# A gated layer by seven block products in place of eight, its last 64 tokens turned

## The chip, the cores and the metric

The kernel runs on one core of a Trainium2 chip. The metric is the device time of one execution in microseconds, taken as the median of three runs. A smaller number is better.

## The reference

Three layers follow each other: attention over a window of 128 tokens, a ReLU layer with a normalization ahead of it, and a gated layer. The change is in the gated layer alone. There are 4 batches (B) of 576 tokens (S), 512 features (DM), and 512 features in each half of the wide layer (DG).

```python
def _moe2_ref(x, w_in, g_ln, w_sg, b_sg, w_out):
    h = x @ w_in                      # (4, 576, 512) @ (512, 1024)
    h = gelu_tanh(h)
    u, v = (h[..., :512], h[..., 512:])
    v_n = (v - mean(v)) / np.sqrt(var(v) + 1e-06) * g_ln
    v_s = np.einsum('ts,bsd->btd', w_sg, v_n) + b_sg[None, :, None]
    gated = u * v_s
    return x + gated @ w_out
```

`gelu_tanh`, `mean` and `var` stand here for the lines that write them out. Below, the four products are called V and U (the two halves of `x @ w_in`), S (the product with `w_sg`, the gate) and O (the product with `w_out`).

## The kernel before

Every large product is made from numbers that are split into a high part (fp32r, names ending in h) and a low part (the rest, names ending in l). A product then has three terms, high by high, high by low and low by high, so each 128 by 128 block of weights meets its data three times. A split costs one ScalarE copy for the high part and one two-input subtraction for the low part.

Attention and the ReLU layer (called phase 1 here) are put in order by a planner, `Sched`: every piece of work is an `Op` with an engine, a cost, a priority, needs and buffers, and the planner writes the instructions in the order in which it thinks they can start. The order on each engine is then fixed in the program. The ReLU layer works on groups of 256 tokens; `m1` (L891) and `m2` (L902) alternate in pieces of 24 matmuls of 256 columns.

The gated layer (phase 2, class `Phase2`) is written out by hand. `play` runs chunks in a given order: V in 18 tiles of 128 tokens (24 matmuls of 256 columns, L1155), U in 16 chunks (24 matmuls, of 256 and 320 columns in turn, L1215), S in 16 chunks of 28 such matmuls (L1230) and O in 16 of 24 (L1257). `early_v` puts V tiles between the last pieces of phase 1. Around them stand GELU (L1201, L1217), the statistics and the normalization of V (L1186 to L1192), the splits (`split`, L1144 on ScalarE, L1145 on GpSimd), the gate (L1234, L1235), the last addition (L1262) and the DMA out (L1263), of which the last chunk makes two, of 320 and of 256 tokens. Weights come in as 64-bit numbers and are turned into high and low parts by `Split64` jobs that `tick` spreads over the chunks. Transfers are issued by SP.

Of the kernel before, what the change touches and what calls it, by code (L numbers as in the profile page):

```python
# [106 lines left out]
def split64(jobs, stage, out=None):  # L107

    for n, j in enumerate(jobs):
        if stage == 0:  # L110
# [17 lines left out]

class Sched:
# [105 lines left out]
def phase1(tc, nc, a, x2d, cst, p2):  # L235
# [599 lines left out]
    def evac(g, j, half, q):  # L835
# [10 lines left out]
        if (g, j) in final:  # L846
            yield Op("SP", 500, q - 1000, token=("xd", g, half), size=2 ** 18)
            sync.dma_start(out=x2d[g][:, zs], in_=x[:, zs])
            if half == 1:
                yield Op(None, 0, 0, need=[("xd", g, 0), ("xd", g, 1)], token=("x2", g))  # L850

    def moe():
        for n, (f, (g, j)) in enumerate(steps):
# [98 lines left out]
    def end_attention():  # L952
# [3 lines left out]
        p2.ps_v = tc.alloc_tile_pool(name="ps_v", bufs=2, space=PSUM, side="right", reuse_waits="tile")  # L956
        p2.open_0()
        sched.done["p2", "wv"] = sched.now
        p2.ps_e = tc.alloc_tile_pool(name="ps_e", bufs=2, space=PSUM, side="right", reuse_waits="tile")
        for n, j in enumerate(list(p2.queue)):  # L960
            sched.spawn(p2.flow(sched, j, n), sched.now)
        for i in range(4):
            sched.spawn(p2.early_v(i, when[2, stream[-1]] + EPRI[i]), sched.now)

# [9 lines left out]
    sched.run("end")  # L974
    for p in (ps_a, ps_h, wps.pop(), np_, cp):
        p.release()
    p2.run(xt[G - 1], (xp, hp))


class Job:  # L980

    def __init__(self, p2, label, name, at, src, shape):
        self.p2, self.label, self.name, self.at, self.src, self.shape, self.stage = p2, label, name, at, src, shape, 0

    def load(self):
        self.s = self.p2.sp.tile([128, 512], I64, tag="st", name="st", bufs=NS2)
        if self.shape:
            self.s = self.s.bitcast(F32)[:, :int(np.prod(self.shape))]  # L990
            if len(self.shape) == 2:
                self.s = self.s.rearrange("p (a b) -> p a b", a=self.shape[0])
        self.p2.nc.sync.dma_start(out=self.s, in_=self.src)

    def step(self):

        if (self.shape or self.stage == 4) and not hasattr(self.p2, self.name):
            return False
        if self.shape:
            self.p2.split(*self.out(), self.s)  # L1000
            return True
        if self.stage == 0:
            self.j = [Split64(self.p2.nc, self.p2.sp, NC2, self.s)]
# [386 lines left out]
```

## Time and profile before

| what | value |
|---|---|
| median of three runs | 732.79 us (732.0 to 733.34) |
| the profiled execution's own time | 731.82 us |
| its span in the profile | 730.1 us |
| TensorE busy | 714.3 us, 98% of the span |
| VectorE busy | 440.0 us, 60% |
| ScalarE busy | 288.5 us, 40% |
| GpSimd busy | 240.4 us, 33% |
| mean granted clock of TensorE | 0.994 |

The span is what the profiler sees between the first and the last instruction; the time of the execution is 1.7 us more. In a row of the chain of waits the first number is the start, the second how long the piece held the chain, then the engine, the tile that it wrote, the line and the number of instructions. In a group a duration is the mean of one instruction, which for matmuls holds their overlap with the next one, so that the pace of matmuls is read from the chain and not from there.

### The profile page before, as it was taken

To read this page: it belongs to the slowest core of one execution; us is meant where nothing else is said; L and a number is where in the kernel's file an instruction comes from. 1 tells how busy PE (TensorE), PEld (TensorE's weight loads), DVE (VectorE), ACT (ScalarE), POOL (GpSimd) and SP (SyncE) were. 2 spreads that over 40 slices of the span, in tenths; PEclk is the share of its full clock that TensorE was granted. 3 is DMA by queue.
4 is the path that set the end of the run, shared out by engine and by line. 5 is a ranking of instruction groups with operands and counts; after the bars stand their busy time and mean duration, and the time that the engine had idled before them with its cause. 6 is when DMAs were issued, how large, how long until landed. Compare 5 with 4: busy or idle time off the path is not lost.

```text
span 730.1 us, 16607 instructions
## 1 busy us (share of the span) xinstructions
PE 714.3 (98%) x6678; PEld 686.9 (94%) x6678; DVE 440.0 (60%) x1202; ACT 288.5 (40%) x762; POOL 240.4 (33%) x291
## 2 busy tenths in 40 slices
PE   6889999999999999999999999999999999999997
PEld 3568999999999999999999999999999999999997
DVE  6999989889782673764744738737325315314232
ACT  5887664545532422522424425124423123223210
POOL 1445251334411321312313233026637217326220
PEclk8999999999999999999999999999999999999999
DMA  8564532033221110112022253305310240250002
GB/s 297 176 209 133 173 121 80 28 94 94 78 87 31 56 51 24 49 58 59 19 69 70 54 165 103 117 29 167 115 64 1 73 137 17 69 175 2 1 33 97
DMA packets 51627, 63.45 MB, mean 87 GB/s; under 512 B 10336, under 2 KB 38880, under 8 KB 51552
## 3 DMA queue, kind: packets, MB, share of 16 engines
q1 hardware_dynamic: 51552, 62.41, 27.2%
q8 instruction: 52, 0.85, 0.5%
q14 instruction: 23, 0.19, 0.1%
HBM read 52.96 MB, written 9.44 MB: 85 GB/s over the span
## 4 chain that ended last, share of the span: by engine, by line
PE 88%; DVE 6%; ACT 3%; DMA 1%; issue 1%; SPq 0%; DVEq 0%; ACTq 0%
PE acc L902 25%; PE ps_h L891 25%; PE ps_s L1230 8%; PE ps_o L1257 7%; PE ps_u L1215 7%; PE ps_v L1155 7%; PE s L476 2%; PE o L661 1%; PE o L617 1%; PE tps L617 1%; ACT t L527 1%; DVE sc L96 1%; PE tps L661 1%; DMA st<-in_w 1%; DVE sc L99 1%
## 5 line engine op out<-in xcount | busy, mean ns | idle before, releaser
L832 DVE SCALAR_TENSOR_TENSOR hl<-ps_h,hh 128x512 fp32r<-128x512 f32 x72 | 49.6, 689 | 84.8 <-ACT hh L830 84.5
L902 PE MATMUL acc<-hh,w2h 128*128 128x256 f32 x576 | 92.5, 283 | 0.0
L891 PE MATMUL ps_h<-xh,w1h 128*128 128x256 f32 x576 | 91.5, 281 | 0.0
L891 PE MATMUL ps_h<-xh,w1l 128*128 128x256 f32 x576 | 90.0, 278 | 0.0
L891 PE MATMUL ps_h<-xl,w1h 128*128 128x256 f32 x576 | 90.0, 278 | 0.0
L902 PE MATMUL acc<-hh,w2l 128*128 128x256 f32 x576 | 89.9, 278 | 0.0
L902 PE MATMUL acc<-hl,w2h 128*128 128x256 f32 x576 | 89.9, 278 | 0.0
L830 ACT ACTIVATE hh<-ps_h 128x512 fp32r<-128x512 f32 x72 | 42.9, 595 | 117.4 <-PE ps_h L891 116.9
L485 POOL TENSOR_SCALAR_AFFINE_SELECT m<-m 128x256 f32<-128x256 f32 (+1 forms) x88 | 41.2, 475 | 124.7 <-ACT m L566 123.1
L891 PEld LDWEIGHTS ps_h<-xh,w1h 128*128 128x128 f32 x576 | 77.1, 188 | 1.2 <-issue 1.1
L902 PEld LDWEIGHTS acc<-hh,w2h 128*128 128x128 f32 x576 | 77.3, 189 | 0.1
L902 PEld LDWEIGHTS acc<-hh,w2l 128*128 128x128 f32 x576 | 77.1, 188 | 0.0
L891 PEld LDWEIGHTS ps_h<-xh,w1l 128*128 128x128 f32 x576 | 77.1, 188 | 0.0
L891 PEld LDWEIGHTS ps_h<-xl,w1h 128*128 128x128 f32 x576 | 77.0, 188 | 0.0
L902 PEld LDWEIGHTS acc<-hl,w2h 128*128 128x128 f32 x576 | 76.9, 188 | 0.0
L527 ACT ACTIVATE t<-t,sm 128x128 f32<-128x128 f32 x144 | 56.1, 392 | 23.4 <-DVE sm L521 22.6
L535 POOL TENSOR_TENSOR t<-t,sm 128x256 f32<-128x256 f32 x47 | 29.6, 629 | 73.4 <-DVE sm L531 53.2
L1234 DVE SCALAR_TENSOR_TENSOR gt<-ps_s,g,bb 128x576 f32<-128x576 f32 x16 | 13.1, 818 | 62.4 <-PE ps_s L1230 62.4
L1145 POOL TENSOR_TENSOR gl<-gt,gh 128x576 fp32r<-128x576 f32 x16 | 23.4, 1466 | 56.4 <-ACT gh L1144 56.4
L87 ACT ACTIVATE sc<-st 128x512 f32<-128x512 f32 (+1 forms) x52 | 30.7, 599 | 20.8 <-DMA st<-in_w 7.6
L99 DVE SCALAR_TENSOR_TENSOR sc<-st,sc 128x512 int32<-128x512 int32 (+1 forms) x52 | 35.6, 691 | 0.2
L96 DVE SCALAR_TENSOR_TENSOR sc<-st,sc 128x512 int32<-128x512 int32 (+1 forms) x52 | 32.7, 637 | 0.2
(177 smaller groups left out, 1561.6 us busy)
## 6 DMA issues: line engine op xcount, KB each, us to landing
st<-in_w SPq DMA_DIRECT2D x24, 512.0 KB, 4.1
x2d<-x SPq DMA_DIRECT2D x18, 256.0 KB, 2.0
out<-xr SPq DMA_DIRECT2D x15, 288.0 KB, 2.1
st<-in_w SPq DMA_DIRECT2D x16, 256.0 KB, 2.6
st<-in_wi SPq DMA_DIRECT2D x8, 512.0 KB, 4.2
st<-x2d SPq DMA_DIRECT2D x8, 512.0 KB, 5.0
xr<-x2d SPq DMA_DIRECT2D x8, 512.0 KB, 7.2
rq<-in_q SPq DMA_DIRECT2D x28, 128.0 KB, 3.0
```

What stands on the lines that cost most here:

```text
L96: dve.scalar_tensor_tensor(out=xi, in0=self.wh, scalar=-0x40000000, in1=xi, op0=ALU.bitwise_and, op1=ALU.bitwise_or)
L99: dve.scalar_tensor_tensor(out=xi, in0=self.wl, scalar=29, in1=xi, op0=ALU.logical_shift_right, op1=ALU.bitwise_or)
L485: pool.affine_select(out=out, in_=in_, pattern=pat, compare_op=ALU.is_ge, fill=0.0, base=-1 if up else 0, channel_multiplier=1 if up else -1)
L527: act.activation(out=t[:, h], in_=t[:, h], func=ACTF.Exp, bias=st[:, h:h + 1], scale=-1.0, accum_out=sums[:, h, 0:1])
L830: act.activation(out=h, in_=ps, func=ACTF.Relu)
L832: dve.scalar_tensor_tensor(out=l, in0=ps, scalar=0.0, in1=h.bitcast(F32), op0=ALU.max, op1=ALU.subtract)
L891: pe.matmul(ps[:, half], w[:, kc, f], m[:, kc], start=kc == 0 and x == 0, stop=kc == 3 and x == 2)
L902: pe.matmul(accs[half][:, d], w[:, f, ds], m[:, k], start=fi and d == 0 and k == 0 and x == 0, stop=la and k == 1 and x == 2, skip_group_c ...
L1155: self.nc.tensor.matmul(ps[:, cs], xs[s][:, kc, c0:c0 + 128], self.wv[m][:, kc, cs], start=kc == 0 and x == 0 and z == 0, stop=kc == 3 and ...
L1215: pe.matmul(ps[:, c], wu[s][:, kc, ds], self.x[m][:, kc, c], start=kc == 0 and x == 0, stop=kc == 3 and x == 2)
L1230: pe.matmul(ps[:, c], l, r[:, c], start=n == 0, stop=n == len(mm) - 1)
L1257: pe.matmul(ps[:, c], wo[s][:, kc, ds], gated[b][m][:, kc, c], start=n == 0, stop=n == 11)
```

## The change

A batch's first 512 tokens and its 512 features are seen as 2 by 2 blocks of 256. V, U and S are made by seven products of sums of such blocks (`PA` and `PB` name the sum of either side, `CHAIN` the order and the PSUM bank), each of 12 matmuls of 256 columns with the three terms. For that the weights and the data are mixed: for every one of the seven sums, additions (L1160), a high part (L1149) and a low part (L1152), the last two lines on ScalarE and on VectorE or GpSimd. Three of the seven products are copied out of PSUM by ScalarE into a room called `te` (L1397), and three are then added on to such a copy by VectorE (L1403); the seventh output is read from PSUM itself.

The 64 tokens that are left of each batch go in other ways. V and U compute them for all four batches together (`v_tail` L1465, `u_tail` L1501, 48 matmuls each, called Vt and Ut). In S, `rest` adds their rows of V to four of the products (L1330, 4 matmuls each). The gate's last 64 rows are computed transposed (`narrow`, L1573 to L1575, 18 matmuls), copied by ScalarE (L1585) and turned back by four fp32 matmuls of 64 columns with a matrix `J` (L1590). O works by groups of 256 tokens, 48 matmuls each; its ninth group is the four times 64 tokens, whose result is sent by DMAs of 64 tokens (L1680).

Phase 2 is now planned by `Sched` too, in the order V0 U0 Vt V1 U1 V2 U2 V3 U3 Ut S0 S1 O0 O1 S2 O2 O3 S3 O4 to O8. Memory is handed out as rooms (`stock`, `take`): X, V and Y rooms for blocks, `te` rooms for sums, `tt` rooms for additions. Six of the Y rooms lie in the memory of the weights of U (`more`) and are handed out when the last product of U3 has been issued. The table of GELU on ScalarE is loaded at the end of attention in place of ahead of V's first tile, O's weights are loaded later, and S's mixed weights lie where V's were.

```diff
+PA = {1: 0, 2: 1, 3: 5, 4: 2, 5: 3, 6: 4, 7: 6}
+PB = {1: 0, 2: 1, 3: 2, 4: 5, 5: 3, 6: 4, 7: 6}
+CHAIN = ((1, "X"), (2, "Z"), (6, "X"), (5, "Y"), (7, "X"), (3, "Y"), (4, "X"))
+TERMS = (0, 0), (0, 1), (1, 0)
...
+        self.order = [("V", 0), ("U", 0), ("Vt", 0)] + [(k, b) for b in range(1, B) for k in "VU"] + [("Ut", 0)]
+        self.order += [("S", 0), ("S", 1), ("O", 0), ("O", 1), ("S", 2), ("O", 2), ("O", 3), ("S", 3)]
+        self.order += [("O", g) for g in range(4, G)]
...
+    def split(self, h, l, src, w, pri, take=(), need=(), make=None, both=True):
...
+        self.nc.scalar.activation(out=h, in_=src, func=ACTF.Copy)
+        o = Op(None, 0, pri, alt=[("POOL", 150 + 2.15 * w, 0)] + [("DVE", 64 + 1.05 * w, DVE2, 1)] * both)
+        yield o
+        self.by(o).tensor_tensor(out=l, in0=src, in1=h.bitcast(F32), op=ALU.subtract)
...
+        for e in range(2):
+            for kt in range(2):
+                for s, m in TERMS:
+                    pe.matmul(ps[:, e], l[s][:, kt, 128 * e:128 * e + 128], r[m][:, kt],
+                              start=fresh and e == 0 and kt == 0 and s == m, stop=kt == 1 and s == 1, skip_group_check=True)
...
+        after = {6: ("e", n, 1), 7: ("e", n, 6), 3: ("e", n, 5), 4: ("a", n, 7)}
+        for k, (P, bk) in enumerate(CHAIN):
...
+            if P == 4 and (kind, b) == ("U", B - 1):
+                for z in "hl":
+                    t = self.pu.tile([128, 3584], F32R, tag="wu" + z, name="more", bufs=1)
+                    for k in range(3):
+                        q = S.stock.setdefault("Y", [])
+                        tok = ("stock", "Y%d" % len(q))
+                        S.done[tok] = S.free["PE"] + HOPP
...
+    def evac(self, kind, b, n, P, ps, te):
+        o = Op("ACT", 490, self.pri(kind, b, -90), need=[("P", kind, b, P)], take=[("te", 1, ("tef", n, P))], token=("e", n, P))
+        yield o
+        te[P] = self.get(o.got[0], [128, 2, 256], F32, "te")
+        self.nc.scalar.activation(out=te[P], in_=ps, func=ACTF.Copy)
...
+        if g < G - 1:
+            yield Op("SP", 500, pri, token=("od", g, i), size=2 ** 18)
+            self.nc.sync.dma_start(out=self.a["out"][b, :, z, 256 * j:256 * j + 256], in_=xr[:, z])
+        else:
+            yield Op("SP", 2000, pri, token=("od", g, i), size=2 ** 18)
+            for b in range(B):
+                self.nc.sync.dma_start(out=self.a["out"][b, :, z, 512:S_], in_=xr[:, z, 64 * b:64 * b + 64])
```

Three places in the program show what this does to the order. A row gives the line, the operation, what it writes and reads, its shape, and the engine on which it waits, if any.

First, ScalarE's order between the last product of U and the first of S. In the kernel before, on the way from U to S of batch 0, GELU of U (`u`) and of V's last tile (`vg`) stand between splits of V (`vnh`, `vt`), and the gate's split (`gh`) comes next:

```order
L1217 ACTIVATE u_7439<-ps_u_7440 128x576 [waits PE_49]
L1144 ACTIVATE vnh_7329<-vg_7415 128x512 [waits DVE_49]
L1217 ACTIVATE u_7439<-ps_u_7474 128x576 [waits PE_49]
L1201 ACTIVATE vg_7528<-ps_v_7503 128x512 [waits PE_49,Pool_49]
L1217 ACTIVATE u_7439<-ps_u_7531 128x576 [waits PE_49]
L1144 ACTIVATE vt0_7020<-vg_7528 64x512 [waits DVE_49]
L1144 ACTIVATE vt1_7021<-vg_7528 64x512
L1217 ACTIVATE u_7439<-ps_u_7562 128x576 [waits PE_49]
L1144 ACTIVATE gh_7593<-gt_7624 128x576 [waits DVE_49]
L1144 ACTIVATE x2h_7016<-st_7627 128x4x256 [waits DMAHW2_49]
```

In the changed kernel, between U3 and S0, `more` is a block of batch 1 of V in U's weights' memory, `bN` a block of normalized V, `tt` and `mx` sums of data and of weights, `wvh` the mixed weights of S, and `te_8632` the copy of S0's first product:

```order
L1149 ACTIVATE more_8501<-v_7601 128x512 [waits PE_49]
L1149 ACTIVATE bN_8539<-tt_8537 128x512 [waits DVE_49]
L1149 ACTIVATE more_8501<-v_7601 128x512
L1149 ACTIVATE wvh_6270<-mx_8443 128x2x256 [waits DVE_49]
L1149 ACTIVATE bN_8573<-tt_8546 128x512 [waits DVE_49]
L1448 ACTIVATE v_8198<-v_8198,ag_8386 128x512
L1149 ACTIVATE bN_8581<-tt_8579 128x512 [waits DVE_49]
L1420 ACTIVATE v_8596<-te_8334 128x2x256
L1420 ACTIVATE v_8596<-te_8318 128x2x256
L1420 ACTIVATE u_8597<-te_8403 128x512
L1420 ACTIVATE u_8598<-te_8464 128x512 [waits PE_49]
L1420 ACTIVATE u_8597<-psU_8372 128x512
L1420 ACTIVATE u_8598<-te_8445 128x512
L1397 ACTIVATE te_8632<-psS_8583 128x512 [waits PE_49,Activation_49]
L1149 ACTIVATE bN_8636<-tt_8623 128x512 [waits DVE_49]
```

The first row waits for TensorE, because Ut still reads U's weights: it is released by Ut's last matmuls. Five more splits, the normalization of a V room and six GELUs stand behind it, and behind those the copy of S0's first product (`psS_8583`). The kernel before has no such copy, and no row here that waits for an earlier reader of a buffer on TensorE.

Second, TensorE's order at the start of S. In the kernel before, U's last matmuls are followed by those of S, whose only waits are for V's splits:

```order
L1215 MATMUL ps_u_7562<-x2h_7016,wuh_6872 128x320
L1215 MATMUL ps_u_7562<-x2l_7017,wuh_6872 128x256
L1215 MATMUL ps_u_7562<-x2l_7017,wuh_6872 128x320
L1215 MATMUL ps_u_7562<-x2h_7016,wul_6873 128x256
L1215 MATMUL ps_u_7562<-x2h_7016,wul_6873 128x320
L1230 MATMUL ps_s_7595<-wsh_7162,vnh_7329 128x256 [waits Activation_49]
L1230 MATMUL ps_s_7595<-wsh_7162,vnh_7329 128x320
L1230 MATMUL ps_s_7595<-wsl_7163,vnh_7329 128x256
L1230 MATMUL ps_s_7595<-wsl_7163,vnh_7329 128x320
L1230 MATMUL ps_s_7595<-wsh_7162,vnl_7330 128x256 [waits Pool_49]
```

In the changed kernel this is the end of S0's second product (into bank `psS_8606`, its last three matmuls those of `rest`) and the start of its third, product 6, into the bank of the first:

```order
L1330 MATMUL psS_8606<-kh_8122,vt0_7342 128x256
L1330 MATMUL psS_8606<-kl_8123,vt0_7342 128x256
L1321 MATMUL psS_8583<-wvh_6270,bN_8573 128x256 [waits Activation_49]
L1321 MATMUL psS_8583<-wvl_6271,bN_8573 128x256
L1321 MATMUL psS_8583<-wvh_6270,bN_8573 128x256 [waits DVE_49]
L1321 MATMUL psS_8583<-wvh_6270,bN_8573 128x256
L1321 MATMUL psS_8583<-wvl_6271,bN_8573 128x256
```

Product 6 waits for ScalarE, which must have copied `psS_8583` out first (the row `te_8632` above), and for VectorE, which makes the low part of `bN_8573`.

Third, SP's order at the end. In the kernel before, the last DMAs send 576 tokens of 128 features each, and the last chunk in two pieces:

```order
L1263 DMA out_0<-xr_8801 128x576 [waits DMAHW6_49,DVE_49]
L1263 DMA out_0<-xr_8801 128x576 [waits DVE_49] x2
L1263 DMA out_0<-xr_9056 128x576 [waits DMAHW3_49,DMAHW4_49,DMAHW2_49,DVE_49]
L1263 DMA out_0<-xr_9056 128x576 [waits DVE_49] x2
L1263 DMA out_0<-xr_9056 128x320 [waits DVE_49]
L1263 DMA out_0<-xr_9056 128x256 [waits DMAHW5_49,DVE_49]
```

In the changed kernel they send 256 tokens of 256 features, and for the ninth group 64 tokens of 256 features, four for each half of the features:

```order
L1676 DMA out_0<-xr_9680 128x2x256 [waits DVE_49]
L1680 DMA out_0<-xr_9736 128x2x64 [waits DMAHW6_49,DMAHW4_49,DVE_49]
L1680 DMA out_0<-xr_9736 128x2x64 [waits DMAHW5_49]
L1680 DMA out_0<-xr_9736 128x2x64
L1680 DMA out_0<-xr_9736 128x2x64 [waits DMAHW7_49]
L1680 DMA out_0<-xr_9736 128x2x64 [waits DMAHW0_49,DVE_49]
L1680 DMA out_0<-xr_9736 128x2x64 [waits DMAHW1_49]
L1680 DMA out_0<-xr_9736 128x2x64 [waits DMAHW2_49]
L1680 DMA out_0<-xr_9736 128x2x64 [waits DMAHW3_49]
```

Behind the last addition there is one DMA in the kernel before; now there are four.

## Rows read from the trace of the kernel before

**Rows 1.** The page: busy us of each engine, share of the span, instructions
```profile
PE 714.3 (98%) x6678; PEld 686.9 (94%) x6678; DVE 440.0 (60%) x1202; ACT 288.5 (40%) x762; POOL 240.4 (33%) x291
```

**Rows 2.** The chain of waits, 480 to 731 us: start us, us, engine, tile, line, instructions
```profile
by line: PE ps_s L1230 23.5%; PE ps_o L1257 20.2%; PE ps_u L1215 20.2%; PE ps_v L1155 20.0%; PE acc L902 7.9%; PE ps_h L891 6.5%; DVE xr L1262 0.2%; DVEq L1386 0.1%; issue 0.0%
...
513.21 2.74 PE ps_v L1155 x24
515.95 2.83 PE acc L902 x24
518.78 8.18 PE ps_v L1155 x72
...
542.43 14.75 PE ps_s L1230 x112
557.18 5.66 PE ps_v L1155 x48
...
701.12 25.30 PE ps_o L1257 x192
...
726.44 0.49 DVE xr L1262
726.92 0.33 DVEq L1386
```

**Rows 3.** Timeline of VectorE, 518 to 520 us: start us, us, instruction
```profile
518.82 0.69 DVE L841 TENSOR_TENSOR et<-acc,rstd 128x512 f32<-128x512 f32 x1 [0.72 <-PE acc L902]
519.42 1.28 DVE L845 TENSOR_TENSOR x<-x,et 128x512 f32<-128x512 f32 x2
```

**Rows 4.** Timeline of ScalarE at 553 us
```profile
553.08 0.69 ACT L1144 ACTIVATE gh<-gt 128x576 fp32r<-128x576 f32 x1 [3.63 <-DVE gt L1235]
553.67 1.04 ACT L1144 ACTIVATE x2h<-st 128x1024 fp32r<-128x1024 f32 x1
```

**Rows 5.** Groups of ScalarE, 513 to 730 us: count, busy us, mean ns of one
```profile
L1144 ACT ACTIVATE vnh<-vg 128x512 fp32r<-128x512 f32 x16 | 10.1, 630 | 29.8 <-DVE vg L1192 29.8
...
L1201 ACT ACT_TABLE_LOAD x1 | 1.3, 1283 | 0.0
```

**Rows 6.** Groups of GpSimd, 513 to 730 us
```profile
L1145 POOL TENSOR_TENSOR vnl<-vg,vnh 128x512 fp32r<-128x512 f32 x16 | 20.8, 1302 | 28.3 <-ACT vnh L1144 28.3
```

**Rows 7.** Groups of VectorE, 513 to 730 us
```profile
L1235 DVE TENSOR_TENSOR gt<-gt,u 128x576 f32<-128x576 f32 x16 | 21.4, 1340 | 1.1
...
L1262 DVE TENSOR_TENSOR xr<-xr,ps_o 128x576 f32<-128x576 f32 x15 | 11.3, 754 | 26.6 <-PE ps_o L1257 26.6
```

**Rows 8.** Timeline at 550 us, VectorE beside GpSimd
```profile
550.01 2.41 POOL L1145 TENSOR_TENSOR x2l<-st,x2h 128x1024 fp32r<-128x1024 f32 x1
...
550.70 2.35 DVE L1235 TENSOR_TENSOR gt<-gt,u 128x576 f32<-128x576 f32 x1
```

**Rows 9.** Windows: window, its length, busy us of PE, PEld, DVE, ACT, POOL, PEclk, DMA, GB/s
```profile
8.00:12.00 4.00, 0.34 (x3) 0.20 (x2) 3.21 (x22) 2.98 (x14) 0.61 (x1) 1.00 1.00 359
12.00:16.00 4.00, 3.62 (x37) 1.88 (x36) 3.55 (x17) 3.60 (x13) 2.02 (x4) 0.50 1.09 385
16.00:20.00 4.00, 3.24 (x16) 1.79 (x16) 2.35 (x15) 2.46 (x11) 0.80 (x3) 0.64 0.93 343
...
44.00:48.00 4.00, 2.09 (x19) 1.21 (x15) 3.93 (x13) 3.57 (x11) 1.65 (x2) 1.00 0.46 115
```

**Rows 10.** Timeline of TensorE, 7 to 13 us, with the idle time before
```profile
11.69 0.44 PE L617 MATMUL tps<-ident,t 128*128 128x128 f32 x2 [3.66 <-POOL t L535]
```

**Rows 11.** Timeline of SP's queue, 725 to 730 us
```profile
726.95 0.81 SPq L1263 DMA_DIRECT2D out<-xr  x2
```

**Rows 12.** DMA issues of the whole run: KB each, median us from issue to landing
```profile
st<-x2d SPq DMA_DIRECT2D x8, 512.0 KB, 5.0
...
out<-xr SPq DMA_DIRECT2D x1, 128.0 KB, 1.8
```

**Rows 13.** Groups of TensorE, whole run: the nearest fp32 matmul
```profile
L723 PE MATMUL ps_ln<-x,ones 128*128 128x256 f32 x8 | 1.9, 379 | 0.0
```

More of the change, by code (lines that the diff above doesn't have):

```diff
@@ L848, in evac @@
             sync.dma_start(out=x2d[g][:, zs], in_=x[:, zs])
+            sched.done["xi", g, half] = sched.now
             if half == 1:
@@ L955, in end_attention, with end_relu @@
             p.release()
[L956 to L963, printed above, removed]
+        p2.begin = ("m1", *stream[-1], 1)
+        p2.open_0(sched)
+    def end_relu():
+        yield Op(None, 0, 0, need=["end", ("xi", G - 1, 0), ("xi", G - 1, 1)])
+        for p in (ps_a, ps_h, wps.pop(), np_, cp, xp, hp):
+            p.release()
+        p2.open_4()
     for e in units:
@@ L973, in phase1 @@
         sched.spawn(gen)
[L974 to L1003, printed above, removed]
[L1004 to L1012 removed]
+    sched.run("finished")
+    p2.close()
+S_ = S
+PA = {1: 0, 2: 1, 3: 5, 4: 2, 5: 3, 6: 4, 7: 6}
+PB = {1: 0, 2: 1, 3: 2, 4: 5, 5: 3, 6: 4, 7: 6}
+CHAIN = ((1, "X"), (2, "Z"), (6, "X"), (5, "Y"), (7, "X"), (3, "Y"), (4, "X"))
+TERMS = (0, 0), (0, 1), (1, 0)
+MM = 113.4
+DVE2 = 100
 class Phase2:
@@ new lines, in tail_v @@
+    def tail_v(self, z, ps, pri):
+        tok = ("vtf", z)
+        o = Op("ACT", 565, pri, need=[("P", "Vt", 0, z)], take=[("te", 1, tok)], token=("bk", "Vt", z))
+        yield o
+        t = self.get(o.got[0], [128, 1, DG], F32, "te")
+        self.nc.scalar.activation(out=t[:, 0], in_=ps.rearrange("p e c -> p (e c)"), func=GELU)
+        yield from self.norm(t, 1, ("vn", z), pri)
+        yield Op(None, 0, pri, need=[("vn", z)])
+        for y in range(2):
+            o = self.vt[2 * z + y] = self.vts[2 * z + y]
+            hi, lo = slice(64 * y, 64 * y + 64), slice(64 - 64 * y, 128 - 64 * y)
+            yield from self.split(o[hi], o[lo], t[hi, 0], 512, pri, both=False)
+            self.sched.done["vt", 2 * z + y] = self.sched.free[self.last] + HOP
+            self.used(tok, 2, self.last)
@@ new lines, in gate @@
+    def gate(self, b, i, j, src, tok, bank, nd, pri):
+        dve, S = self.nc.vector, self.sched
+        g = 2 * b + j
+        o = Op("DVE", 680, pri, need=nd, take=[("te", 1, ("gf", b))] if bank else [])
+        yield o
+        t = src
+        if bank:
+            t = self.get(o.got[0], [128, 2, 256], F32, "te")
+        for e in range(2):
+            d = 2 * i + e
+            dve.scalar_tensor_tensor(out=t[:, e], in0=src[:, e], scalar=self.g2[:, d:d + 1], in1=self.bb[:, 256 * j:256 * j + 256],
+                                     op0=ALU.mult, op1=ALU.add)
+        if bank:
+            S.done[tok] = S.free["DVE"] + HOP
+            tok = ("gf", b)
+        o = Op(None, 0, pri, alt=[("POOL", 150 + 2.15 * 512, 0), ("DVE", 602, DVE2, 1)], need=[("ur", g)])
+        yield o
+        self.by(o).tensor_tensor(out=t, in0=t, in1=self.u[g][:, 2 * i:2 * i + 2], op=ALU.mult)
+        self.used(("uf", g), 2, o.eng)
+        yield from self.split(None, None, t, 512, pri, take=[("V", 1, ("Gf", b, i, j))], make=lambda z: self.make(("G", b, j), i, z))
+        S.done["G", b, i, j] = S.done[tok] = S.free[self.last] + HOP
@@ L1340, in body @@
         p2 = Phase2(tc, nc, a, x2d, mh)
+        p2.ident = ident
         phase1(tc, nc, a, x2d, (ident, ones, onesr, g1, mh, far), p2)
```

828 lines of the change are left out of this document (565 added, 263 removed).

## The prediction

> **What bounds the kernel now.** I read the page's busy line first: TensorE is busy 98% of the span, the next engine 60% [rows 1]. So the time is TensorE's work plus what holds it up. The chain of waits over the last 250 us shows how this stands in the stage that is changed [rows 2]. From 513.21 us to the end of O at 726.41 us (701.12 + 25.30) piece follows piece on TensorE without a wait; 2.83 of it is the last piece of phase 1. The gated layer is thus 213.2 - 2.83 = 210.4 us of matmuls, and then a tail of 3.7 us to the end of the span: last addition, DMA issue, landing. Any matmul saved comes off the end, as long as the other engines keep up, and every new wait of TensorE is added in full.
>
> **The price of a matmul.** In the same rows a matmul of 256 columns takes two values: 8.18 us for 72 is 113.6 ns, 5.66 us for 48 is 117.9 ns. Both last over many instructions and neither has a wait in it; what chooses between them I cannot see. All V pieces together are 20.0% of the 250.1 us of that view, 50.0 us for 18 x 24 = 432 matmuls, or 116 ns [rows 2]. I take 116, since V is the one product of the stage made of 256 columns alone, and keep 113.6 and 117.9 as ends.
>
> **What is removed and added on TensorE.** Counted from the order, the changed stage has 3 x 4 x 7 x 12 = 1008 matmuls in products, 96 in Vt and Ut, 64 in `rest`, 72 in `narrow` and 9 x 48 = 432 in O: 1672 of 256 columns. At 116 ns that is 194.0 us (189.9 and 197.1 at the ends). To this come 16 fp32 matmuls of 64 columns that turn the gate's tail. The nearest row has 256 columns, 8 in 1.9 us, so 0.24 each [rows 13]; a quarter of the columns costs between a quarter of that and all of it, 1.0 to 3.8 us in all; I take half, 1.9. The sum is 195.9 us, so TensorE's own work falls by **14.5 us** (11.4 at 117.9 ns, 18.6 at 113.6).
>
> **The wait at S0.** ScalarE's row `more_8501` waits for Ut's last matmuls, and all that follows in its queue waits too. Put the end of Ut at 0. A ScalarE copy of 576 starts the next after 0.59 us [rows 4], so I take 0.55 for 512 in a row and 0.63 for the last one of a row [rows 5]. A two-input VectorE operation starts the next after 0.60 and ends after 0.69 [rows 3]; hand-overs between engines are small beside that (553.05 to 553.08, the end of a VectorE row to the copy that it releases) [rows 4, 8].
> - `wvh`, fourth in ScalarE's queue, ends at 3 x 0.55 + 0.63 + 0.05 = 2.3. VectorE's low part of it stands ahead of the low part of `bN_8487`, which ends at 2.3 + 0.60 + 0.69 = 3.6. TensorE does product 1 (12 x 0.117 = 1.4) and two matmuls of product 2, to 1.6, and waits **2.0 us** for that low part. It then does the other 14 to 5.3.
> - VectorE goes on with another low part and `tt_8579`, which ends at 2.3 + 3 x 0.60 + 0.69 = 4.8; ScalarE's `bN_8581` waits for it. Behind it stand six GELUs and then the copy `te_8632`: start 4.8 + 7 x 0.55 = 8.7, end 9.3. Product 6 may not start before, so TensorE waits from 5.3 to 9.3, **4.0 us**.
>
> Together 6.0 us. The bounds: 2 us if the GELUs and the copy were quicker or TensorE were later than I think, 9 us if GpSimd or VectorE hold the splits up as well.
>
> **Other waits.** Between the first product of S1 and O0 the order has 14 VectorE operations of two SBUF inputs and 3 from PSUM (17 x 0.60 = 10.2 us), 8 gate operations of half that width (2.4), about 1.5 of statistics, and 5 of GpSimd, at 1.30 each [rows 6] 6.5. While a GpSimd operation ran, a VectorE operation took 2.35 in place of about 0.75 [rows 7, 8]. If the two never overlap, S1's vector work is 20.6 us against 118 matmuls or 14 us, which leaves 6 us that can become waits, unless O0 and O1 (96 matmuls, 11 us, little vector work) absorb them. V and U are lighter, worked out in the same way: 15 to 18 us for 15 to 20 us of matmuls. I take 0.5 us for S1 and 0.5 for U0 and the rest: **1.0**, bounds 0 and 6.
>
> The Trainium skill, "SBUF — State Buffer", section "SBUF: two separate sides", says that VectorE with two SBUF inputs and GpSimd take a shared port pair in turn, each for a whole instruction. The trace agrees, with the 2.35 us; by this rule the vector work adds up as above, and by plain overlap S1 would have no wait at all.
>
> **The tail.** Now the last addition is one of 512 (0.69) where the last had been 320 and then 256, and four DMAs follow where one did. Two DMAs took SP 0.81 us to issue, 0.40 each [rows 11]. Before, the last was issued by 727.76; now 726.44 + 0.69 + 4 x 0.40 = 728.7. Landing I leave at 1.8 us [rows 12]. **+0.95 us**, bounds 0.3 and 1.5.
>
> **What costs nothing.** GELU's table (1.3 us of ScalarE [rows 5]) moves under the matmuls of phase 1, where ScalarE, busy 40% of the span [rows 1], has room; uncovered it would cost at most that. The blocks of x are loaded a batch ahead, 5 us [rows 12] against 15 or more of matmuls. The many mixings of weights and data lie under V and U by the loads above.
>
> **Sum.** 731.82 - 14.5 + 6.0 + 1.0 + 0.95 = 725.3 us for this profiled execution's own time. The median shown is 0.97 above it, so I forecast **726.3 us**. Differences within 0.2% (1.5 us) I count as no change, about what a measurement of this kernel can tell.
>
> **Rivals.**
> - *The clock falls after S0's wait.* After TensorE had waited 3.66 us [rows 10] the granted clock was 0.50 from 12 us, and 0.64 in the four us behind: half speed (1.2 in place of 2.4 GHz) until about 18.9 [rows 9]. After shorter waits it stayed at 1.00, with TensorE busy 2.09 of 4 us [rows 9]. S0's 4.0 us lies nearer to the first of these. At half speed for as long as there (7 us) or half of it, the stage loses 3.5 or 1.7: 729.8 or 728.0. The Trainium skill, "TensorE: Matmul & The Clock Gate", section "HAM oscillation — how this bites in real kernels", tells of just this, bursts that each begin slowly since the wait ahead of them brought the clock down; the row at 12 us agrees, and by it the sum is 728.9 in place of 726.3. Against it: 1.64 us of work lies between the two waits. 0.26.
> - *All matmuls at the quick pace*, 113.6 ns: 4.0 less, 722.3. For it: the longest V piece had it. 0.10.
> - *All at the slow pace*: 3.1 more, 729.4, or 731 with a microsecond or two of the waits above their estimate. 0.10.
> - *The change doesn't gain*: the vector work of S1 is paid in full, 6 us, or the S0 wait is 9: 731.5 to 734. 0.07.
> - *Slower*: the pair of VectorE and GpSimd sets the pace. The stage has 33 two-input operations of GpSimd of 256 or more; each can hold VectorE up by 1.340 - 0.754 = 0.59 us [rows 7], 19.4 in all. From 14 of them whose delay reaches a product, 8.2 us is added, and the time is above 734.3; with 20 it is 738. For it: VectorE gets 36 additions of products and about 100 two-input operations of mixing and splitting here. Against it: TensorE has other products between most sums. 0.09.
>
> **How the numbers follow.** The forecast itself, 724 to 728, has 0.38. Faster by over 0.2% (below 731.3): 0.38 + 0.26 + 0.10 and 0.08 of the slow pace, 0.82. Within: 0.07 + 0.02 = 0.09. Slower: 0.09. The range is 721.5 to 731.3: it leaves out the last two rivals, 0.02 of the slow pace and 0.02 at the quick pace's lower end, 0.2 in all.
>
> **What would show it.** In the profile after: TensorE's products in phase 2 about 196 us; a wait of some 4 us on L1321 that ends with ScalarE's L1397, and one of 2 us that ends with VectorE's L1152, both near the start of S0, with ScalarE idle ahead of L1149 until TensorE's L1501 is done; granted clock at 1.00 or 0.50 behind; few other waits, at S1; four DMAs of L1680 at the end. Wrong would make me: no wait at S0 (then about 720), waits at each S and U that end with VectorE, or matmuls of 256 columns outside 113 to 118 ns.

## The result and the profile after

The changed kernel is slower. Its median is 737.08 us (735.47 to 739.27, 5 runs); the kernel before has 732.79 (730.91 to 733.34, 5 runs). The ratio is 1.0068 with a 95% interval of 1.0042 to 1.0094. The profiled execution took 737.08 us, with a span of 735.3 and a mean granted clock of 0.990. The forecast was 726.3, 10.8 us below.

The page's busy line of the changed kernel, which answers to [rows 1]:

```profile
PE 707.6 (96%) x6734; PEld 678.0 (92%) x6734; DVE 524.8 (71%) x1396; ACT 342.0 (47%) x873; POOL 194.0 (26%) x257
```

TensorE is busy 6.7 us less, but the span is 5.2 us longer: TensorE now stands still for longer than it saves. VectorE has 85 us more work and ScalarE 54 more, and yet both have room on the average. The waits of TensorE in the gated layer, 505 to 736 us, with what ended them (us in total, times, longest):

```profile
PE psS L1321 <- ACT te L1397: 3.5, 1, 3.5
PE psU L1321 <- ACT te L1397: 3.3, 4, 1.5
PE psS L1321 <- DVE bN L1152: 1.9, 1, 1.9
PE psV L1321 <- ACT te L1397: 1.8, 2, 0.9
PE psU L1321 <- DVE te L1403: 0.6, 1, 0.6
```

The first and third row are the two waits at S0 that were forecast. The others stand in V and U, where half a microsecond had been allowed, and all but 0.6 us of those listed end with the same ScalarE row: the copy of a product out of PSUM. (The list counts from the end that the profile gives a matmul, 0.28 us after its start. Counted from the starts, and with the shortest, as in the table below, those of V and U come to 8.3 us.) In the chain of waits, which before was TensorE alone [rows 2], other engines now appear (480 to 736 us):

```profile
571.24 1.06 ACT te L1397 x2
...
618.33 1.13 ACT v L1420 x2
619.46 2.04 ACT u L1420 x4
622.04 4.55 PE psS L1321 x24
...
702.03 28.28 PE psO L1660 x240
```

The last row gives the pace of matmuls without a wait, 28.28 / 240 = 117.8 ns. The row at 622.04 has 24 matmuls in 4.55 us, or 190 ns each.

**S0.** ScalarE's timeline there, which answers to [rows 4]:

```profile
613.03 0.63 ACT L1149 ACTIVATE more<-v 128x512 fp32r<-128x512 f32 x1 [4.80 <-PE psUt L1501]
...
617.79 0.63 ACT L1149 ACTIVATE bN<-tt 128x512 fp32r<-128x512 f32 x1 [1.34 <-DVE tt L1160]
618.33 1.13 ACT L1420 ACTIVATE v<-te 128x512 f32<-128x512 f32 x2
619.37 1.13 ACT L1420 ACTIVATE u<-te 128x512 f32<-128x512 f32 x2
...
621.40 0.58 ACT L1397 ACTIVATE te<-psS 128x512 f32<-128x512 f32 x1
```

ScalarE stood idle for 4.80 us until Ut's last matmul, then did the splits, waited for VectorE's sum, did six GELUs, and copied S0's first product at 621.40, 8.4 us after Ut; the forecast had 8.7. TensorE waited 2.06 and 3.68 us by the starts of its matmuls. Behind that the clock fell. Windows (window, its length, busy us of PE, PEld, DVE, ACT, POOL, PEclk, DMA, GB/s), as in [rows 9]:

```profile
620.00:622.00 2.00, 0.00 (x0) 0.00 (x0) 1.97 (x4) 2.00 (x5) 0.00 (x0) 0.99 0.00 0
622.00:623.00 1.00, 0.96 (x4) 0.97 (x5) 0.95 (x2) 1.00 (x3) 0.00 (x0) 0.50 0.00 0
...
625.00:626.00 1.00, 1.00 (x9) 1.00 (x9) 1.00 (x3) 0.60 (x1) 0.00 (x0) 0.82 0.00 0
626.00:628.00 2.00, 2.00 (x20) 2.00 (x19) 2.00 (x5) 1.31 (x3) 0.00 (x0) 1.00 0.00 0
```

From 622.0 to about 625.4 the granted clock was 0.50, the lower level of 1.2 GHz (0.82 from 625 to 626 is 0.36 us of it). Most matmuls there start every 213 ns in place of 117; the 18 of them cost 1.7 us.

**V and U.** One of the waits that the forecast did not have, at U of batch 1, on VectorE and then on ScalarE:

```profile
557.38 0.69 DVE L1152 TENSOR_TENSOR bX<-xf,bX 128x512 fp32r<-128x512 f32 x1
557.98 0.69 DVE L1160 TENSOR_TENSOR tt<-xf,tt 128x512 f32<-128x512 f32 x1
558.58 0.68 DVE L1403 TENSOR_TENSOR te<-te,psU 128x512 f32<-128x512 f32 x1
```

```profile
559.30 0.63 ACT L1420 ACTIVATE u<-te 128x512 f32<-128x512 f32 x1 [1.58 <-DVE te L1403]
559.84 0.61 ACT L1149 ACTIVATE bX<-tt 128x512 fp32r<-128x512 f32 x1
560.36 0.58 ACT L1397 ACTIVATE te<-psU 128x512 f32<-128x512 f32 x1
```

The copy at 560.36 needs only its own product, which was done at 558.46. But ScalarE's order is fixed, and the first of the three rows, a GELU, waits 1.58 us for VectorE's sum. The sum's product was done at 557.05, but it stands behind a subtraction and an addition for later data. TensorE had its last matmul at 559.60 and the next at 560.99. One row that waits holds up others that could run; over V and U, VectorE was busy 74.0 of the 97 us from 516 to 613, and ScalarE 66.8.

**The tail.** SP's queue, as in [rows 11]:

```profile
728.22 4.73 SPq L1680 DMA_DIRECT2D out<-xr  x8
```

Eight DMAs keep SP issuing until 732.95, 1.93 us behind the end of the last addition (730.33 + 0.69), where the forecast had 4 x 0.40 = 1.60. From TensorE's end (730.3) to the span's end it is 5.0 us, where it was 3.7.

### The profile page after: what moved, and what is told of

It is laid out like the page before. It is cut to its first block, busy times and chain, and to the rows that moved or that the text cites. A ratio compares the mean times of both kernels' runs of the same rounds, so it can differ in the third digit from the quotient of the medians.

```text
span 735.3 us, 17050 instructions
## 1 busy us (share of the span) xinstructions
PE 707.6 (96%) x6734; PEld 678.0 (92%) x6734; DVE 524.8 (71%) x1396; ACT 342.0 (47%) x873; POOL 194.0 (26%) x257
## 4 chain that ended last, share of the span: by engine, by line
PE 77%; DVE 10%; ACT 7%; DMA 3%; issue 2%; SPq 0%; POOL 0%; ACTq 0%; DVEq 0%; POOLq 0%
PE ps_h L889 26%; PE acc L900 25%; PE psO L1660 7%; PE psS L1321 5%; PE s L475 2%; PE o L660 1%; ACT t L526 1%; PE tps L616 1%; DMA st<-in_w 1%; DVE te L1403 1%; PE o L616 1%; DVE bX L1152 1%; DMA xf<-x2d 1%; PE psS L1330 1%; DVE bs L1436 1%
## 5 line engine op out<-in xcount | busy, mean ns | idle before, releaser
L1660 PE MATMUL psO<-bG,woh 128*128 128x256 f32 x256 | 45.4, 281 | 0.0
L1321 PE MATMUL psU<-bX,wuh 128*128 128x256 f32 x224 | 40.3, 282 | 4.0 <-ACT te L1397 3.3
L1321 PE MATMUL psV<-wvh,bX 128*128 128x256 f32 x224 | 40.5, 279 | 1.9 <-ACT te L1397 1.8
L1660 PEld LDWEIGHTS psO<-bG,woh 128*128 128x128 f32 x256 | 39.1, 188 | 0.0
L1321 PEld LDWEIGHTS psU<-bX,wuh 128*128 128x128 f32 x224 | 34.2, 189 | 5.0 <-ACT te L1397 4.1
```

The lines of the kernel that those rows point to most:

```text
L1321: pe.matmul(ps[:, e], l[s][:, kt, 128 * e:128 * e + 128], r[m][:, kt], start=fresh and e == 0 and kt == 0 and s == m, stop=kt == 1 and s = ...
L1660: nc.tensor.matmul(ps[:, e], self.wo[s][:, kc, ds], r, start=e == kc == 0 and s == m, stop=kc == 3 and s == 1, skip_group_check=True)
```

## The experiments

Three theories were to be told apart. **A**: the wait lies in the order of the in-order queues of ScalarE and VectorE; copies of products stand behind GELUs, splits and conversions that wait. **B**: VectorE and GpSimd hold each other up. **C**, for the last runs: whatever else is edited, fewer two-input operations on GpSimd are what helps.

For each run the table gives the ratio to the kernel before, and from its profile the waits of TensorE in V, U and S. They are worked out from the starts of consecutive matmuls: what lies beyond 117 ns, where it is over 150. Matmuls at half clock (200 to 218 ns apart) are counted apart. S includes the waits of the turn-back. In these profiles the first matmul of V starts between 515.05 and 518.33 us, so a microsecond between two medians can arise ahead of the gated layer; where two intervals overlap, a step from one run to the other is not shown by the time alone.

| kernel | median us | ratio (95% interval) | waits V / U / S, us | at half clock |
|---|---|---|---|---|
| the change | 737.08 | 1.0068 (1.0042 to 1.0094) | 2.85 / 5.45 / 6.11 | 18 |
| e1_rooms | 733.67 | 1.0022 (1.0011 to 1.0033) | 2.84 / 5.39 / 4.57 | 4 |
| e2_order | 729.98 | 0.9975 (0.9962 to 0.9988) | 0.49 / 3.28 / 3.18 | 4 |
| e3_both | 729.68 | 0.9964 (0.9951 to 0.9978) | 0.49 / 3.32 / 2.39 | 3 |
| e4_no_gpsimd | 740.66 | 1.0124 (1.0100 to 1.0149) | 8.11 / 1.68 / 5.62 | 61 |
| e5_costs | 735.82 | 1.0048 (1.0029 to 1.0066) | 0.18 / 6.69 / 5.00 | 17 |
| e6_hold | 735.53 | 1.0041 (1.0025 to 1.0057) | 0.53 / 5.74 / 6.44 | 3 |
| e7_tail | 728.68 | 0.9948 (0.9933 to 0.9964) | 0.50 / 3.34 / 2.37 | 4 |
| e8_queue | 721.81 | 0.9862 (0.9842 to 0.9883) | 0.44 / 0.28 / 0.25 | 4 |
| e9_wo | 727.54 | 0.9931 (0.9919 to 0.9944) | 0.22 / 3.83 / 2.13 | 4 |
| e10_copy | 726.40 | 0.9913 (0.9900 to 0.9925) | 0.79 / 2.56 / 2.69 | 5 |
| e11_pool | 723.99 | 0.9881 (0.9867 to 0.9895) | 0.38 / 2.04 / 1.20 | 3 |
| e12_vector | 734.06 | 1.0032 (1.0015 to 1.0049) | 5.77 / 0.45 / 3.71 | 27 |

All of them compute the whole reference. Where the edit moves code, lines after it have other numbers: the copy L1397 is L1389 in most, the addition L1403 is L1395.

### e1_rooms: S0's rooms handed out later

The block that hands out `more` goes from U3's product 4 (the lines with -) to the end of Ut, behind its last matmul (those with +).

```diff
-            if P == 4 and (kind, b) == ("U", B - 1):
-                for z in "hl":
-                    t = self.pu.tile([128, 3584], F32R, tag="wu" + z, name="more", bufs=1)
...
+        for z in "hl":
+            t = self.pu.tile([128, 3584], F32R, tag="wu" + z, name="more", bufs=1)
...
```

> The six rooms in the memory of U's weights are handed out behind Ut, so no row of ScalarE waits for Ut's last matmuls. Theory A (the waits of TensorE come from rows that stand in front of the copies in the in-order queues, as the planner put them): the two waits at S0 of the changed kernel, 5.8 us, fall to 2 us or less, the granted clock stays at 1.00 behind them (1.6 us back), the 8.2 us of waits in V and U stay as they are, and some 2 us come back at S1: 731 to 734 us. Rival B (VectorE and GpSimd hold each other up and set the pace): the waits only move, 735 to 738 us.

Measured: 733.67 us, 3.4 less than the change. With the rooms handed out behind Ut, the planner no longer places a split into them at the head of ScalarE's queue. Both of S0's long waits are gone, the clock stays up, and S keeps 4.57 us of shorter waits. V and U keep theirs to 0.1 us. So the forecast wait was real and was worth some 3 us with the clock behind it, and it is not all that made the kernel slow: e1 is still 0.2% slower than the kernel before.

### e2_order and e3_both: the planner's order

```diff
-                key = (start + TRADE * min(max(op.pri, -99), 99), op.pri, n)
+                key = (start + TRADE * min(max(op.pri, -99), 99) + op.late, op.pri, n)
...
-        o = Op(None, 0, pri, alt=[("POOL", 150 + 2.15 * w, 0)] + [("DVE", 64 + 1.05 * w, DVE2, 1)] * both)
+        o = Op(None, 0, pri, alt=[("POOL", 250 + 2.15 * w, 0)] + [("DVE", 64 + 1.05 * w, DVE2, 1)] * both)
...
-        o = Op("ACT", 490, self.pri(kind, b, -90), need=[("P", kind, b, P)], take=[("te", 1, ("tef", n, P))], token=("e", n, P))
+        o = Op("ACT", 560, self.pri(kind, b, -90), need=[("P", kind, b, P)], take=[("te", 1, ("tef", n, P))], token=("e", n, P))
...
-        yield Op("ACT", 565, pri, need=nd + [("ua", 2 * b + j) if kind == "U" else ("va", b, j)], token=tok)
+        yield Op("ACT", 565, pri, need=nd + [("ua", 2 * b + j) if kind == "U" else ("va", b, j)], token=tok, late=200)
...
-            yield Op("ACT", 710, pri, token=tok if e == E - 1 else None)
+            yield Op("ACT", 810, pri, token=tok if e == E - 1 else None)
```

e2 has this edit alone: GELUs are held back by 200 ns in the planner's order, and three of its costs are raised towards the traced ones (GpSimd's for additions too). e3 has e1's edit as well.

> Same instructions, other order: the planner's costs in phase 2 are set nearer to the trace (copy out of PSUM 560 in place of 490 ns, normalization on ScalarE 810 in place of 710, GpSimd 100 ns more), and GELU of V and U is held back by 200 ns, so that copies and splits go first. The rooms in U's weights are handed out as in the changed kernel. Theory A: the waits in V and U fall from 8.2 us to 3 or less, those at S0 and S1 are 4 to 6 us: 727 to 731 us. Rival B: the vector work is the same and so is the time, 735 to 738 us.

> Both edits together. Theory A: all waits of TensorE in phase 2 together fall from 14 us to 5 or less, the clock stays at 1.00, and the time is 722 to 728 us, below the kernel before. Rival B: 733 to 738 us.

Measured: 729.98 and 729.68 us. The same operations are 7.1 us faster than in the change, and V's and U's waits fall from 8.3 to 3.8 us, not to the 3 expected. It is not the order alone that differs: the higher cost of GpSimd also moves work, and of its 34 two-input operations of 256 elements or more 24 are left. e5 below tells the two apart. The two edits don't add: e2 alone also shortens S0's wait, so little is left for e1. The 722 to 728 expected of e3 was missed; the longest wait that stayed, 2.0 us, is at U0. ScalarE's timeline in e3:

```profile
527.10 0.66 ACT L84 ACTIVATE sc<-st 128x512 f32<-128x512 f32 x1 [3.35 <-DMA st<-in_wo]
527.67 0.62 ACT L1412 ACTIVATE v<-te 128x512 f32<-128x512 f32 x1
529.31 0.63 ACT L1412 ACTIVATE v<-te 128x512 f32<-128x512 f32 x1 [1.03 <-DVE te L1395]
529.85 0.64 ACT L84 ACTIVATE sc<-st 128x512 f32<-128x512 f32 x1
530.40 0.58 ACT L1412 ACTIVATE v<-psV 128x512 f32<-128x512 f32 x1
530.88 0.62 ACT L1149 ACTIVATE bX<-xf 128x512 fp32r<-128x512 f32 x1
531.39 0.59 ACT L1389 ACTIVATE te<-psU 128x512 f32<-128x512 f32 x1
```

Here a conversion of O's weights, needed 115 us later, waits 3.35 us for its transfer. A GELU behind it waits another 1.03 us for VectorE's sum, and the copy of U0's product stands behind both. That the transfer is the cause is tested in e9.

### e4_no_gpsimd: the pair of VectorE and GpSimd

```diff
-        o = Op(None, 0, pri, alt=[("POOL", 150 + 2.15 * w, 0)] + [("DVE", 64 + 1.05 * w, DVE2, 1)] * both)
+        o = Op(None, 0, pri, alt=[("POOL", 99999, 0)] + [("DVE", 64 + 1.05 * w, DVE2, 1)] * both)
...
-        o = Op(None, 0, pri, alt=[("POOL", 150 + 2.15 * 512, 0), ("DVE", 602, DVE2, 1)], need=[("ur", g)])
+        o = Op(None, 0, pri, alt=[("DVE", 602, DVE2, 1)], need=[("ur", g)])
```

(and the same in the two other places where the planner chooses between these engines in the gated layer).

> The changed kernel with the planner's choice between GpSimd and VectorE taken away: all two-input operations of phase 2 but the low parts of V's tail go to VectorE, so hardly any of them can be held up by GpSimd. Rival B: at least the 5 us by which VectorE operations were stretched come back, 729 to 733 us. Theory A: VectorE, which has 25 operations of 0.6 us more and no other order of its waits, is no better, 735 to 741 us.

Measured: 740.66 us, slower. Of GpSimd's 34 two-input operations of 256 elements or more, 4 are left, and what VectorE's two-input operations take beyond 0.70 us, summed over their rows, falls from 6.1 us to 2.1. B asks for a gain of some microseconds. Instead VectorE's queue grew: V waits 8.11 us, most of it for VectorE's low parts, and the waits in all are 15.4 us against 14.4. The clock fell too, 61 matmuls at half of it against 18, which is about 4 us and most of what this profile (744.66 us, the slowest of six) has more inside the layer. So the run says that without the pair the waits do not shrink; how much slower they alone would be it does not say. In e3 the sum is 5.8 us, about that of the change, at 7.4 us less time. B is not the main thing that makes the change slow.

It has a part, though. In the change, GpSimd and then VectorE ahead of a wait of V:

```profile
568.06 1.29 POOL L1152 TENSOR_TENSOR wol<-sc,woh 128x512 fp32r<-128x512 f32 x1 [1.85 <-ACT woh L1149]
```

```profile
568.28 1.10 DVE L1440 TENSOR_SCALAR ag<-ag 128x2 f32<-128x2 f32 x1
569.29 0.68 DVE L1403 TENSOR_TENSOR te<-te,psV 128x512 f32<-128x512 f32 x1
```

The small operation takes 1.10 us beside GpSimd's subtraction, where it takes 0.17 at 580.69. The sum behind it is late by that, and so are a GELU and two copies on ScalarE (571.24 above); TensorE waits 1.1 us before 571.87. In the same way an addition of 256 elements takes 1.54 us at 603.24 beside a subtraction of GpSimd (602.99, 1.51 us) in place of 0.42, and TensorE waits 0.8 us before 605.77. These are 1.9 of the 8.3 us in V and U.

### e5_costs and e6_hold: the two halves of e2

e5 has e2's edit without `late` (no row held back); e6 has `late` without the costs.

> One half of e2_order alone: the three costs of the planner (560, 810, GpSimd 100 ns more), GELU not held back. Theory A as sharpened (what hurts is a GELU that waits for VectorE and stands in front of a copy): with the GELUs where they were, most waits stay, V and U 6 to 9 us, S0 4 us or more: 732 to 738 us. If the costs were what mattered, 727 to 731.

> The other half alone: GELU of V and U held back by 200 ns in the planner's choice, its costs as in the changed kernel. If holding GELU back were enough, 727 to 731 us. If both halves are needed, since the planner with too low costs still believes that a GELU's sum is done in time, 732 to 738.

Measured: 735.82 and 735.53 us. Each half gains 1.3 to 1.6 us, which the intervals do not tell from nothing, and the two together 7.1. Both clear V of most waits (0.18 and 0.53) and leave 5 to 6.7 us in U and in S. e5 leaves GpSimd as many operations as e2, 24, and its edit lacks nothing but the holding back of GELU. Between the two lie 5.8 us, so here the order by itself is worth about that much. Without the new costs the same hold gains only 1.6 us (e6, with 36 operations on GpSimd); how far this comes from the costs and how far from the division of work is not shown. No single number of the planner is at fault.

### e7_tail: the last two groups of O exchanged

```diff
-        self.order += [("O", g) for g in range(4, G)]
+        self.order += [("O", g) for g in (4, 5, 6, 8, 7)]
```

On top of e3, so that the group with the eight small DMAs is not the last.

> e3_both with the group of the four times 64 tokens one place earlier, so that the last thing sent is one DMA of 256 KB in place of four of 64 KB. From the end of TensorE to the end of the span the changed kernel took 5.0 us against 3.7 before; here 3.9 to 4.3, and the time 0.7 to 1.2 us below e3_both, 728.5 to 729.0. If landing of the larger DMA eats it, no change.

Measured: 728.68 against 729.68 us, 1.0 less; the intervals overlap, but the profile shows where it comes from. TensorE's end to the span's end is 4.1 us in place of 5.0. The tail's term was of the right kind.

### e8_queue: transfer, copies and engines

On top of e7: the transfer of O's weights may start early, and only the conversion waits for its room; the copies of products move 300 ns forward in the planner's order; GpSimd is costed 650 ns higher, so that it gets fewer splits and additions (the cost is raised for both); and three other costs change.

```diff
-        nd = [("room", "late")] if w == "wo" else []
+        nd = []
...
-        ahead = [("mt", "wu", 1)] if w == "wo" else [("mt", w, 0)] if kc % 2 else [("mt", "wv", 1)] if w == "wu" else []
+        ahead = [("mt", "wu", 1), ("room", "late")] if w == "wo" else [("mt", w, 0)] if kc % 2 else [("mt", "wv", 1)] if w == "wu" else []
...
-        o = Op("ACT", 560, self.pri(kind, b, -90), need=[("P", kind, b, P)], take=[("te", 1, ("tef", n, P))], token=("e", n, P))
+        o = Op("ACT", 560, self.pri(kind, b, -90), need=[("P", kind, b, P)], take=[("te", 1, ("tef", n, P))], token=("e", n, P), late=-300)
...
-        o = Op(None, 0, pri, alt=[("POOL", 250 + 2.15 * w, 0)] + [("DVE", 64 + 1.05 * w, DVE2, 1)] * both)
+        o = Op(None, 0, pri, alt=[("POOL", 900 + 2.15 * w, 0)] + [("DVE", 64 + 1.05 * w, DVE2, 1)] * both)
...
-MM = 113.4
+MM = 115.0
-DVE2 = 100
+DVE2 = 50
-        o = Op("ACT", 110 + .82 * w, pri, need=need, take=take)
+        o = Op("ACT", 140 + .82 * w, pri, need=need, take=take)
```

> e7_tail with O's weights transferred before the stage begins (their first ScalarE row waited 3.4 us for the transfer, at the head of its queue, and U0's third product 2.2 us for the copy behind it), copies of products drawn 300 ns ahead, and two-input work kept on VectorE unless GpSimd is far ahead. Theory A: waits of TensorE in phase 2 of 4 us or less in all: 724 to 728 us. If U0's wait has another cause than that transfer, it stays and the time is 727 to 730.

Measured: 721.81 us, better than the 724 to 728 expected, 10.4 less than the kernel before measured beside it, and 15.3 less than the change. This is the version that beats both by most. The waits of TensorE in its gated layer, listed as above, are an empty list (1.0 us by the starts); pieces of its chain of waits:

```profile
541.66 8.48 PE psV L1321 x72
...
582.27 8.18 PE psV L1321 x72
...
631.05 0.84 PE psN L1589 x8
...
687.82 28.28 PE psO L1659 x240
```

Again piece follows piece on TensorE, as in [rows 2]. The two paces of before are both still there: 8.48 / 72 = 117.8 ns and 8.18 / 72 = 113.6.

### e9_wo, e10_copy, e11_pool: e8's edits apart

e9 is e7 with the edit of the transfer; e10 is e9 with the copies 300 ns forward; e11 is e7 with GpSimd's 900 ns and `DVE2` = 50 alone.

> The version with the order, the rooms and the tail, with one edit more: the transfer of O's weights may start earlier, so that the conversion on ScalarE no longer waits for it ahead of U0's copies. Theory A (ScalarE's queue, what stands ahead of a copy): only the 2.0 us wait at U0 goes, 728.7 becomes about 726.7; S0's 1.2 us wait and the turn-back's 0.7 stay. Theory C (the version with every edit gained by putting fewer two-input operations on GpSimd): about 728.5, the wait at U0 only moves to another copy.

> The version before, with the copies of products moved 300 ns forward in the planner's order as well. Theory A: S0's wait of about 1.2 us goes or shrinks below 0.4, the time is 725 to 726.5. Theory C: no change against the version before, within 1 us.

> The version with the order, the rooms and the tail, with one edit: GpSimd's splits and additions are costed at 900 ns more overhead in place of 250, so that the planner gives most of them to VectorE; O's weights and the copies as they were. Theory A: the 2 us wait at U0 behind the transfer stays, 728 to 729.5. Theory C: the larger part of the 6.9 us between this version and the one with every edit is had by this alone, 722 to 724.5.

Measured: 727.54, 726.40 and 723.99 us. e9 gained 1.1 of the 2.0 us: U0's wait shrank to 0.6, so the transfer was most of its cause, but two others of 1.1 to 1.2 us came elsewhere in U. e10 gained another 1.1. Neither step is clear of noise, and the waits in all hardly move, from 6.2 us in e7 to 6.2 and 6.0. The two expectations put e7's wait of 1.2 us at S0; its trace has it at S1 (before 629.89, where S1 began at 625.26). S0 has one of 1.4 us in e9 and of 2.0 in e10, both for a copy. So A named the right kind of cause and not the next row in the way.

e11 fell where C had put it, 4.7 us below e7 without the other edits. Of this, 2.6 us are waits (6.2 to 3.6), and 1.3 lie ahead of the layer, whose first matmul starts at 515.05 us in place of 516.33. GpSimd has 12 two-input operations of 256 elements or more in place of 24. How much of the gain is the pair itself? At S0 in e7, GpSimd and then VectorE:

```profile
609.81 2.25 POOL L1152 TENSOR_TENSOR bN<-v,bN 128x512 fp32r<-128x512 f32 x1 [7.03 <-ACT bN L1149]
```

```profile
609.61 0.68 DVE L1160 TENSOR_TENSOR tt<-v,tt 128x512 f32<-128x512 f32 x1
610.21 2.39 DVE L1152 TENSOR_TENSOR bN<-tt,bN 128x512 fp32r<-128x512 f32 x2
```

Two subtractions of VectorE take 2.39 us beside one of GpSimd; alone two take 1.28 to 1.29 in the same stretch. That is 1.1 us of VectorE's time, but not of the kernel's: TensorE is busy all 5.00 us from 608 to 613. Over the layer the lengthening falls from 5.8 us to 2.0. Since e11 also moves rows in the queues, what part of the 4.7 us is the pair and what part the order stays open. The parts add here: e10's 2.3 and e11's 4.7 make 7.0, and e8 is 6.9 below e7.

### e12_vector: e8 without GpSimd

e8 with e4's edit: VectorE alone has the splits, the additions and the gate.

> The version with every edit, and besides none of phase 2's two-input operations of 256 or more elements on GpSimd, which leaves VectorE alone with them. Theory A (queues and their order; VectorE has room): the time is that of the version with every edit, 720.5 to 724, with at most 3 us of waits of TensorE in phase 2. Rival B (the pair of VectorE and GpSimd holds products up): faster by up to 2 us, 719 to 720. If GpSimd's help is needed for the vector work, as it was in the order before the edits, S0 gets waits of several us and the time is above 725.

Measured: 734.06 us, 12.3 slower than e8. The forecasts of A (720.5 to 724) and of B both missed; it is the third case, above 725. Nine operations of 256 or 512 elements changed their engine (in e8 GpSimd still had seven of the gate, a split and an addition). The waits are 9.9 us in place of 1.0, and 27 matmuls at half clock in place of 4 add about 2. The longest waits of its TensorE:

```profile
PE psV L1321 <- DVE bX L1152: 4.4, 2, 3.5
PE psS L1321 <- DVE more L1152: 2.7, 1, 2.7
```

and VectorE ahead of the first of them:

```profile
562.62 1.28 DVE L1428 BATCH_NORM_STATS2 bs<-v 128x6 f32<-128x512 f32 x2
565.38 0.25 DVE L1431 BATCH_NORM_AGGREGATE ag<-bs 128x2 f32<-128x6 f32 x2 [1.49 <-ACT te L1440]
565.66 0.17 DVE L1432 TENSOR_SCALAR ag<-ag 128x2 f32<-128x2 f32 x1
565.74 0.68 DVE L1152 TENSOR_TENSOR bX<-xf,bX 128x512 fp32r<-128x512 f32 x1
```

VectorE stands idle for 1.49 us at an aggregation that waits for ScalarE's normalization, and the low part of `bX`, for which TensorE waits, is queued behind it. It is the pattern of S0 and U0 on another engine: work behind a row that waits. C falls as a rule ("fewer on GpSimd is better"), and so does B as the main cause: twice, taking GpSimd out made the kernel slower.

## Why the prediction was wrong

The forecast's own sum was 725.3 us and the profiled execution took 737.1. From the first matmul of V to the last of O the forecast has 195.9 us of matmuls and 7.0 of waits, 202.9; measured are 214.3 (515.75 to 730.02). The 11.4 us between them, by its steps:

- **"What costs nothing" and "Other waits" failed.** The mixings of weights and data were to "lie under V and U by the loads above", with 0.5 us for "U0 and the rest". V and U wait 8.3 us: **+7.8**. The step compared sums, so much vector work against so many matmuls, and sums have no order in them. The queues do: e2, where copies come ahead of GELUs and ten operations leave GpSimd, takes 4.5 us out of V and U, e8 all but 0.7. From e5 to e2, with as many operations on GpSimd, the GELUs' place alone is worth 5.8 us of time. The pair of VectorE and GpSimd stands behind 1.9 of the 8.3 us.
- **The wait at S0 was right**: 2.06 and 3.68 against 2.0 and 4.0, by the mechanism told. All of S, with 0.5 for S1, was put at 6.5 and has 6.1: **-0.4**.
- **The clock** was a rival with 0.26. It came: 18 matmuls at half clock, **+1.7**, the size given there for half of the stretch. The Trainium skill, "TensorE: Matmul & The Clock Gate", section "HAM oscillation — how this bites in real kernels", describes such a burst that begins slowly behind a wait. The windows at 622 us agree, with 0.50.
- **The turn-back** was mis-sized: 3.2 us in place of 1.9, **+1.3**, within its bounds of 1.0 and 3.8, but partly by luck. The trace has two rows for each fp32 matmul, 32 for the 16. The 8 rows of [rows 13] are four matmuls in the program, so a matmul of 256 columns costs 0.47 us and not 0.24; one of 64 columns costs 0.20.
- **The pace** was 116.7 ns in the mean where nothing waits, not 116: **+1.0**.
- **The tail** has 1.3 us in place of 0.95, **+0.35** outside of the 11.4: SP took 1.93 us to issue behind the last addition, not 1.60.

The rival that ended on the slower side put the price on the pair of VectorE and GpSimd. The result is its time (734 to 738), but in the main not by its mechanism, so that the agreement is chance: e4 and e12 take the pair apart and are slower. The lengthened rows add up to 6.1 us on VectorE, an engine that also waits; on TensorE, 1.9 us of waits in V and U could be followed back to such rows. The Trainium skill, "SBUF — State Buffer", section "SBUF: two separate sides", holds for single rows here (2.39 us for two in place of 1.28).

Among the signs named as ones that would make the forecast wrong, waits at S and U that end with VectorE are close to what came; they end with ScalarE's copies, which at U1 and at S0 stand behind a row that waits for VectorE. Without waits the gain is there: e8 spends 200.1 us on the gated layer and is 10.4 us faster than before. What it lacks to the forecast's 14.5 is mostly the turn-back and the pace (117.0 ns in e8).

## What to carry to other kernels

When a kernel gives up matmuls for additions, copies and splits, don't compare sums of work: go along each in-order queue and ask, for every row on which TensorE waits, what stands ahead of it and what that waits for. Where a planner sets the order, small changes of its costs (490 or 560 ns for a copy) move rows past each other. The order, and which of two engines does an operation, were worth some 14 us here (15.3 with the tail's 1.0), more than the 12 us of matmuls that the change saved (210.4 before, 198.2 in the change without waits and slow clock); how the 14 divide between the two is not shown. Such repairs need not add up: e1 and e2 together gain less than the sum, e5 and e6 more, and in e9 and e10 another row takes the place of the one moved.

## What the runs showed of the hardware

- The clock fell to 0.50 for 3.4 us behind waits of 2.06 and 3.68 us with 1.6 us of work between; ahead of the first wait TensorE had been full with Ut's matmuls, 47 in 5.59 us.
- A ScalarE normalization with a scale and a bias from SBUF, of 128 x 512, takes 0.80 us, a copy of the same size 0.58 to 0.60 out of PSUM and 0.62 to 0.63 from SBUF to fp32r (L1448, L1397 and L1149 of the change).
- A VectorE operation on 128 x 2 elements took 1.10 us beside a GpSimd subtraction of 1.29 and 0.17 without one.
- An fp32 matmul shows as two rows: 16 of 64 columns are 32 rows and took 3.2 us, 0.20 us each.
- 256-column matmuls run at 113.6 or 117.8 ns for tens of instructions in a row, before and after the change; no run here shows what chooses.
